# First 512 tokens as chunks of 128 and 384, in a fused polynomial-attention and rational-MLP kernel

## The chip, the cores and the metric

The kernel runs on one core of one Trainium2 chip. The metric is the device time of one execution in microseconds, taken as the median of several executions. The profile is of one further execution, recorded by the hardware profiler. The engines are PE (TensorE, matmuls into PSUM), ACT (ScalarE), DVE (VectorE), POOL (GpSimd) and SP (SyncE, which issues DMAs).

## The reference, cut to what matters

Four batches, four heads, 1088 positions and 32 features per head go through a linear attention with a product feature map, and the result (4352 tokens of 128 features) through a layer of 2048 hidden units with a rational activation.

```python
def phi(x):                                   # r = 8
    a = np.einsum('rd,bhsd->bhsr', S1, x)
    b = np.einsum('rd,bhsd->bhsr', S2, x)
    return np.einsum('bhsi,bhsj->bhsij', a, b).reshape(*x.shape[:-1], r * r)
q_p, k_p = phi(q), phi(k)
kv = np.einsum('bhsf,bhsd->bhfd', k_p, v);  z = np.sum(k_p, axis=2)
num = np.einsum('bhsf,bhfd->bhsd', q_p, kv)
den = np.einsum('bhsf,bhf->bhs', q_p, z)[..., None] + 1e-06
x = (num / den) transposed to (tokens, 128)
...
h = x @ w_in                                  # 128 -> 2048
P = a[0] + a[1]*h + a[2]*h**2 + a[3]*h**3
Q = 1.0 + abs(b[0])*abs(h) + abs(b[1])*h**2
out = (P / (Q + 1e-6)) @ w_out                # 2048 -> 128
```

## The kernel before, in words

**Order.** The kernel is a list of steps. `Plan.add` (line 67) notes for each step its engine, an estimated duration, what it comes after and which buffers it takes and gives back; `Plan.issue` (line 73) then issues the steps in the order of the hand-kept list `ORDER` (line 19). Every engine therefore works in the order in which its instructions come out of that list. An instruction that waits holds up all that stand behind it on its engine.

**Keys.** For each batch, `add_keys` (line 433) turns k into features: PE transposes (line 445), ACT copies the transposed keys from PSUM (449), PE projects them by S1 and S2 (454), ACT copies (461), DVE forms the products k_p (472). PE then sums k_p against v, with a column of ones for z (489). DVE spreads the sums into block matrices kv_bd and z_bd (544 to 552), PE projects z by S2 (557), and DVE writes the projected z into the third part of the query weights, W_abc for whole chunks (566) and W_rem for the remainder (563). W_abc has two places, used by batches of even and odd number.

**Queries.** `add_queries` (line 584) makes x for a chunk of tokens. Chunks have 512 tokens, two per batch, and one remainder chunk takes the last 64 positions of all four batches. The regular path: PE transposes q (595), ACT copies it (599), PE projects by W_abc to a, b and a third part c with which the denominator is a sum over eight products (605), ACT copies abc (615), DVE makes the denominator and scales a by its inverse (626, 630, 634, 638), then forms the products q_p (643), PE transposes them (651), ACT copies (657), PE multiplies by kv_bd straight into transposed x (663), ACT copies xT (712). Both chunks of a batch other than the first share one denominator pass.

The first 512 tokens go another way, as two chunks of 256 (labels 0 and 0b, the `early` branch). Their projection needs only S1 and S2, not z. After the product and its transposes, PE multiplies with the numerator and denominator columns of kv_bd side by side (676, with 1e-6 put in by 669), DVE inverts and divides (687, 693), PE transposes the result to x (701) and ACT copies xT (708). The loads of q for these two chunks come separately on SP (line 218).

**Hidden layer.** `add_group` (line 776) handles a group: one chunk and some of the 16 slices of 128 hidden units, up to 4096 columns in all (tokens times slices). PE makes h into PSUM tiles of 1024 columns (822; two such tiles exist), ACT, for some tiles DVE, casts it to bf16 into `hb` (828; `CASTS`, line 159, names groups whose seventh and eighth slices DVE casts). On `hb` DVE takes the absolute value u (837) and the square lin (845; on ACT, 843, for groups whose plan has an s), then y = lin*a3 + a1 (849), y *= hb (855). Q adds lin to u; ACT forms 1/Q as exp(-ln(...)) through the tile L (859, 862). P adds lin + a0 (852) to y, then y *= u (855), and PE multiplies by w_out (875). The two additions run on DVE (907), or, for groups whose entry in `PLANS` (line 158) has Q or P, as an accumulating DMA that POOL issues (911). A z in the plan lets PE add a0 through a second product with w_out instead of line 852. The groups of chunk 0 are of 2, 2, 4 and 8 slices of 256 tokens (`FIRST`, line 156) and lie packed in one set of buffers; chunk 0b is one group of 16 slices; all other chunks of 512 tokens have two groups of 8 slices; the remainder chunk has 8, 4, 3 and 1 slices of 256 tokens (`LAST`).

**Buffers.** Line 178 counts them: three each of hb, u, lin and y, one L, three w_ps tiles in PSUM for the attention part, one each of qT, abc, q_p and den. w_out is loaded as float32 into the buffer of L (196, 261). ACT scales it to w_out_b, POOL to w_out_0 (426, 427), and L is given back after that.

`HOT` (line 162) lists matmuls on zeros that fill PE's gaps (1036); they stand in `ORDER` too.

Of the kernel before, what the change touches and what calls it, by code (L numbers as in the profile page):

```python
# [12 lines left out]
FP = mybir.dt.float32  # L13
BF = mybir.dt.bfloat16
# [109 lines left out]
def kernel(  # L124
# [36 lines left out]
    XWARM = (0, 0)  # L161
# [34 lines left out]
    w_out_l = tile_of(moe, "L", [128, LW], FP)[:, :NF * d_model]  # L196
    w_out_f = w_out_l.rearrange("p (n d) -> p n d", d=d_model)
# [8 lines left out]
    def load_main(eng, name, src, b, part=None):  # L206
# [7 lines left out]
        if name == "q_sb" and part is not None:  # L214
            flat = T[name, b].rearrange("p h j d -> p (h j d)")
            if part < 1:
                for i in (int(2 * part),):
                    QUEUE[eng].dma_start(out=flat[:, i * 256:(i + 1) * 256].rearrange("p (h j d) -> p h j d", h=H, j=2),
                                         in_=src[:, :, 2 * i:2 * i + 2, :])
# [57 lines left out]
    ld["q", 0] = load("SP", lambda e: load_main(e, "q_sb", q, 0, 0), 128, rank=-97.5, take=["kq"])  # L277
# [3 lines left out]
    ld["q", 0, 0.5] = load("SP", lambda e: load_main(e, "q_sb", q, 0, 0.5), 128, rank=-96.7)  # L281
# [4 lines left out]
    ld["wo"] = load("SP", load_wo, 800, rank=-93, take=["L"])  # L286
# [15 lines left out]
    mask4 = consts.tile([128, H], FP, name="mask4")  # L302
    mask2 = consts.tile([128, 2], FP, name="mask2")
# [16 lines left out]
    den_e = consts.tile([128, 2, 4, 2], FP, name="den_e")  # L320
# [60 lines left out]
    c_s2 = plan.add("POOL", 250, s_expanded, after=[ld["s"], c_pool], rank=-3)  # L381
    c_sw = {}
# [48 lines left out]
    plan.add("DVE", 1, lambda: None, after=c_w + c_w0, rank=-0.1, give=["L"])  # L431

    def add_keys(b, rank):
# [141 lines left out]
        zs = plan.add("DVE", 200, lambda: z_spread(False), after=[zp, c_sw[b % 2]], rank=rank + 0.05, name=f"zspread {b}")  # L575
# [8 lines left out]
    def add_queries(n, nt, srcs, weights, kv_lhs, load_steps, kv_steps, w_steps, rank, give=(), early=False,  # L584
# [23 lines left out]
        def evac_abc():  # L608
# [5 lines left out]
            if nt == JC or early:  # L614
# [52 lines left out]
        def den_eps(t):  # L667
            T["nd", n, t] = tile_of(aps, "w_ps", [128, CW], FP)
            nc.tensor.matmul(nd_parts(t)[0][:, :, 2 * D:], lhsT=ident,
                             rhs=den_t[n % BUFS["den"]][:, 0:8, R].rearrange("p (g h) -> p g h", h=2), start=True, stop=False,  # L670
                             skip_group_check=True)

        def num_den(t, hp):
            for i in range(2):
                j = 2 * t + i
                nc.tensor.matmul(T["nd", n, t][:, (i * NP + hp) * 66:(i * NP + hp + 1) * 66],
                                 lhsT=T["q_pT", n][:, hp, j * 128:(j + 1) * 128],
                                 rhs=kv_lhs(hp)[0][2], start=False, stop=True, skip_group_check=True)

        def nd_parts(t):  # L680
            nd = T["nd", n, t][:, :4 * 66].rearrange("p (g c) -> p g c", g=4)
            den = den_e[:, n]
            return nd, den

        def div_inverse(t):
# [386 lines left out]
```

## Time and profile before

| | |
|---|---|
| median of 3 runs | 248.33 us (248.24 to 248.41) |
| the profiled execution | 248.28 us |
| its span, first to last instruction | 246.3 us |
| granted TensorE clock | 1.000 |
| busy: PE, DVE, ACT, POOL | 238.5, 222.9, 222.8, 55.0 us |
| POOL's DMA queue, share of 16 engines' span | 69.3% |

The span is from the first to the last instruction; the execution has some 2 us around it. A line of a timeline gives the start and the duration in microseconds, the engine, the line of the source, the operation, output and inputs with their shapes, how many instructions are merged (an f32 matmul that isn't a transpose appears as two passes), and in brackets the idle time of the engine before it with what ended it. A line of groups gives the busy time in us and the mean ns of one after the first bar, and after the second the idle time ahead of the group. Durations of instructions that follow each other on an engine overlap slightly, so start to start is the better measure for a row of them.

### The profile page before, as it was taken

To read this page: it belongs to the slowest core of one execution; us is meant where nothing else is said; L and a number is where in the kernel's file an instruction comes from. 1 tells how busy PE (TensorE), PEld (TensorE's weight loads), DVE (VectorE), ACT (ScalarE), POOL (GpSimd) and SP (SyncE) were. 2 spreads that over 40 slices of the span, in tenths; PEclk is the share of its full clock that TensorE was granted. 3 is DMA by queue.
4 is the path that set the end of the run, shared out by engine and by line. 5 is a ranking of instruction groups with operands and counts; after the bars stand their busy time and mean duration, and the time that the engine had idled before them with its cause. 6 is when DMAs were issued, how large, how long until landed. Compare 5 with 4: busy or idle time off the path is not lost. (4 is left out here: it accounts for less than half of the span.)

```text
span 246.3 us, 3019 instructions
## 1 busy us (share of the span) xinstructions
PE 238.5 (97%) x1119; PEld 140.3 (57%) x1129; DVE 222.9 (90%) x239; ACT 222.8 (90%) x201; POOL 55.0 (22%) x69
## 2 busy tenths in 40 slices
PE   7999999999999999999999999999999999999985
PEld 3889987566648556545654554444444446644442
DVE  0743898999999999999999999999999999999982
ACT  3236799989999999999999989999999999999993
POOL 7817000201130111151111112131132211111100
DMA  6897700497995498989999899999999999999742
GB/s 168 277 316 168 252 3 1 74 210 163 214 178 100 79 194 148 183 158 186 184 193 183 154 183 208 210 170 187 186 186 184 181 229 193 190 174 175 130 130 64
DMA packets 21662, 41.65 MB, mean 169 GB/s; under 512 B 5504, under 2 KB 12688, under 8 KB 21520
## 3 DMA queue, kind: packets, MB, share of 16 engines
q0 software_dynamic: 8000, 30.43, 69.3%
q1 hardware_dynamic: 13360, 10.95, 14.7%
q8 instruction: 9, 0.15, 0.3%
q10 hardware_dynamic: 288, 0.08, 0.2%
q14 instruction: 5, 0.04, 0.0%
HBM read 8.82 MB, written 2.23 MB: 45 GB/s over the span
## 5 line engine op out<-in xcount | busy, mean ns | idle before, releaser
L822 PE MATMUL h_ps<-xT,w_in_sb 128*128 128x512 f32 (+1 forms) x320 | 127.1, 534 | 0.7 <-ACT hb L828 0.7
L822 PEld LDWEIGHTS h_ps<-xT,w_in_sb 128*128 128x128 f32 x320 | 57.1, 190 | 42.3 <-issue 33.8
L828 ACT CAST hb<-h_ps 128x1024 bf16<-128x1024 f32 (+3 forms) x62 | 61.4, 1009 | 4.3 <-PE h_ps L822 4.0
L859 ACT ACTIVATE L<-u,kappa 128x4096 f32<-128x4096 bf16 (+5 forms) x23 | 65.0, 2830 | 0.3 <-DMA u<-lin 0.3
L862 ACT ACTIVATE u<-L 128x4096 bf16<-128x4096 f32 (+5 forms) x23 | 63.0, 2749 | 0.1
L911 POOL DMA_DIRECT2D u<-lin x16 | 22.3, 1395 | 99.8 <-DVE u L837 26.6
L855 DVE TENSOR_TENSOR y<-y,u 128x4096 bf16<-128x4096 bf16 (+5 forms) x23 | 39.6, 1729 | 0.9 <-ACT u L862 0.8
L855 DVE TENSOR_TENSOR y<-y,hb 128x4096 bf16<-128x4096 bf16 (+5 forms) x23 | 39.6, 1724 | 0.2
L845 DVE TENSOR_TENSOR lin<-hb 128x4096 bf16<-128x4096 bf16 (+5 forms) x22 | 37.3, 1702 | 2.2 <-ACT hb L828 2.1
L911 POOL DMA_DIRECT2D y<-lin x14 | 17.5, 1251 | 69.4 <-DVE lin L852 19.6
L875 PE MATMUL out_ps<-y,w_out_b 128*128 128x512 bf16 (+1 forms) x138 | 30.1, 354 | 1.4 <-DVE y L855 1.1
L849 DVE TENSOR_SCALAR y<-lin,a_t 128x4096 bf16<-128x4096 bf16 (+5 forms) x23 | 24.4, 1062 | 0.4 <-PE out_ps L875 0.3
L875 PEld LDWEIGHTS <-w_out_b 128*128 128x128 bf16 x144 | 14.0, 98 | 18.4 <-issue 7.0
L837 DVE TENSOR_SCALAR u<-hb 128x4096 int16<-128x4096 int16 (+5 forms) x23 | 21.6, 941 | 0.7 <-ACT hb L828 0.6
L489 PEld LDWEIGHTS w_ps<-v_aug,k_p 128*128 128x128 f32 x128 | 15.1, 192 | 2.5 <-issue 2.2
L489 PE MATMUL w_ps<-v_aug,k_p 128*128 128x96 f32 x128 | 15.6, 276 | 0.0
L852 DVE TENSOR_SCALAR lin<-lin,a_t 128x4096 bf16<-128x4096 bf16 (+5 forms) x17 | 15.3, 902 | 0.0
L657 ACT COPY q_pT<-w_ps 128x512 f32<-128x512 f32 (+1 forms) x20 | 10.5, 558 | 3.8 <-PE w_ps L651 3.8
L643 DVE TENSOR_TENSOR q_p<-abc 128x1024 f32<-128x1024 f32 (+1 forms) x10 | 10.6, 1062 | 1.1 <-ACT abc L615 1.0
L875 PE MATMUL out_ps<-u,w_out 128*128 128x512 bf16 x46 | 11.2, 379 | 0.3 <-ACT u L862 0.2
L472 DVE TENSOR_TENSOR k_p<-ab 128x1024 f32<-128x1024 f32 x8 | 9.8, 1234 | 1.7 <-ACT ab L461 1.7
L1036 PE MATMUL w_ps<-const-float32-0.0 128*128 128x512 bf16 x47 | 11.1, 381 | 0.1
(111 smaller groups left out, 221.1 us busy)
## 6 DMA issues: line engine op xcount, KB each, us to landing
u<-lin POOLq DMA_DIRECT2D x15, 1024.0 KB, 9.0
y<-lin POOLq DMA_DIRECT2D x13, 1024.0 KB, 8.9
v_aug<-in_v_dram SPq DMA_DIRECT2D x8, 256.0 KB, 4.2
out_dram<-oT SPq DMA_DIRECT2D x7, 256.0 KB, 5.2
kq<-in_k_dram SPq DMA_DIRECT2D x3, 512.0 KB, 4.3
kq<-in_q_dram SPq DMA_DIRECT2D x3, 512.0 KB, 7.1
w_in_sb<-in_moe_w_in_dram SPq DMA_DIRECT2D x1, 1024.0 KB, 6.0
kq<-in_k_dram SPq DMA_DIRECT2D x2, 256.0 KB, 3.3
```

The costliest lines, as they stand in the source:

```text
L489: nc.tensor.matmul(T["kv", b][:, hp * 96:(hp + 1) * 96], lhsT=lhs(hp), rhs=rhs(hp), start=(first and hp == 0), stop=final, skip_group_chec ...
L822: nc.tensor.matmul(T["h", g, s][:, i * W:(i + 1) * W], lhsT=w_in_sb[:, fi * 128:(fi + 1) * 128], rhs=T["xT", n][:, :W], start=True, stop=True)
L828: copy(out=T["t", g][:, s * W:(s + nsub) * W], in_=T["h", g, s][:, :nsub * W])
L837: nc.vector.tensor_scalar(out=u().bitcast(mybir.dt.int16), in0=ht().bitcast(mybir.dt.int16), scalar1=0x7FFF, scalar2=None, op0=AX.bitwise_and)
L845: nc.vector.tensor_mul(out=sq(), in0=ht(), in1=ht())
L849: nc.vector.tensor_scalar(out=y(), in0=sq(), scalar1=a_t[:, 3:4], scalar2=a_t[:, 1:2], op0=AX.mult, op1=AX.add)
L852: nc.vector.tensor_scalar(out=sq(), in0=sq(), scalar1=a_t[:, 0:1], scalar2=None, op0=AX.add)
L855: return lambda: nc.vector.tensor_mul(out=out(), in0=in0(), in1=in1())
L859: nc.scalar.activation(out=T["L", g][:, :gw], in_=u(), func=ACT.Ln, bias=1.0 + 1e-6, scale=kappa[:, 2:3])
L862: nc.scalar.activation(out=u(), in_=T["L", g][:, :gw], func=ACT.Exp, scale=-1.0)
L875: nc.tensor.matmul(T["o", n][:, :W], lhsT=w[:, fi, :], rhs=T[src, g][:, i * W:(i + 1) * W], start=(start and i == 0), stop=(stop and i == ...
L911: nc.gpsimd.dma_start(out=dst(), in_=src(), accum_op=AX.add, max_dma_last_dim=GW)
```

## The change

The first 512 tokens are split into 128 and 384. The 128 go the early way, now with one product, one division and one transpose. The 384 (label 0b) go the regular query path with their own denominator. Its weights need z of batch 0 for three 128-token columns only; they are put into batch 1's place of W_abc, with a mask built by POOL (`mask12`), and batch 1's own spread is ordered behind the projection of the 384 tokens. The q loads are 64 and 192 KB instead of twice 128 KB.

The groups change with the chunks: 4, 4 and 8 slices of 128 tokens, then two groups of 8 slices of 384 tokens (3072 columns), 512, 512, 1024, 3072 and 3072 columns where there were 512, 512, 1024, 2048 and 4096. A PSUM tile of h holds two slices of 384, each in a bank of its own, so a cast takes 768 columns. Group 3 adds Q and P by DMA, group 4 as before squares on ACT and adds both by DMA, group 8 adds only Q by DMA, and group 11 no longer casts on DVE. w_out is loaded into a buffer of y instead of L, and y is given back when both scalings are done. `ORDER` is a new list for all steps; `HOT` keeps its counts.

```diff
-    FIRST = [2, 2, 4, 8]
+    HEAD = 1
+    FIRST = [4, 4, 8]
     LAST = [8, 4, 3, 1]
-    PLANS = {**{g: "QP" for g in range(4, 20)}, 5:"Q",17:"Qz",**{g:"QPz" for g in (13,15,16,18)},4:"sQP",14:"QPz"}
-    CASTS = {18:(6,),16:(6,),14:(6,),12:(6,),17:(6,),13:(6,),15:(6,),11:(6,)}
+    PLANS = {**{g: "QP" for g in range(4, 20)}, **{g:"Q" for g in (5,8)},11:"QP",14:"QPz",17:"Qz",**{g:"QPz" for g in (13,15,16,18)},3:"QP",4:"sQP"}
+    CASTS = {18:(6,),16:(6,),14:(6,),12:(6,),17:(6,),13:(6,),15:(6,)}
...
-    w_out_l = tile_of(moe, "L", [128, LW], FP)[:, :NF * d_model]
-    w_out_f = w_out_l.rearrange("p (n d) -> p n d", d=d_model)
+    w_out_l = tile_of(moe, "y", [128, 2 * NF * d_model], BF)
+    w_out_f = w_out_l.bitcast(FP).rearrange("p (n d) -> p n d", d=d_model)
...
-    ld["q", 0] = load("SP", lambda e: load_main(e, "q_sb", q, 0, 0), 128, rank=-97.5, take=["kq"])
+    ld["q", 0] = load("SP", lambda e: load_main(e, "q_sb", q, 0, 0), 64, rank=-97.5, take=["kq"])
...
-    ld["q", 0, 0.5] = load("SP", lambda e: load_main(e, "q_sb", q, 0, 0.5), 128, rank=-96.7)
+    ld["q", 0, 0.5] = load("SP", lambda e: load_main(e, "q_sb", q, 0, 0.5), 192, rank=-96.7)
...
+    def pool_mask12():
+        nc.gpsimd.tensor_copy(out=mask12.rearrange("p h j -> p (h j)").rearrange("p (i m) -> p i m", m=H),
+                              in_=mask4[:, None, :].broadcast_to([128, JC - HEAD, H]))
...
-    plan.add("DVE", 1, lambda: None, after=c_w + c_w0, rank=-0.1, give=["L"])
+    plan.add("ST", 1, lambda: None, after=c_w + c_w0, rank=-0.1, give=["y"], name="used w_out")
...
+        def z_piece():
+            nc.vector.tensor_mul(
+                out=W_abc[:, 1, 0:JC - HEAD].rearrange("p i m r -> p (i m) r")[:, :, 2 * R:R3].rearrange("p (h j) r -> p h j r", h=H),
+                in0=T["zp", b][:, :H * R].rearrange("p (h i) -> p h i", h=H)[:, :, None, :].broadcast_to([128, H, JC - HEAD, R]),
+                in1=mask12[:, :, :, None].broadcast_to([128, H, JC - HEAD, R]))
+
+        if b == 0:
+            T["w_step", "piece"] = zp = plan.add("DVE", 170, z_piece, after=[zp, c_sw[1], c_m12], rank=rank + 0.05, name="zpiece")
+        zs = plan.add("DVE", 200, lambda: z_spread(False), after=[zp, c_sw[b % 2], T["q abc", 1] if b == 1 else None], rank=rank + 0.05, name=f"zspread {b}")
...
+        def both_transposes():
+            T["qpTp", n] = tile_of(aps, "w_ps", [128, CW], FP)
+            qp = T["q_p", n][:, :H, :].rearrange("p h f -> p (h f)")
+            for hp in range(NP):
+                nc.tensor.transpose(T["qpTp", n][:, hp * 128:(hp + 1) * 128], in_=qp[:, hp * 128:(hp + 1) * 128], identity=ident)
...
-                nc.tensor.matmul(T["h", g, s][:, i * W:(i + 1) * W], lhsT=w_in_sb[:, fi * 128:(fi + 1) * 128],
+                nc.tensor.matmul(T["h", g, s][:, i * step:i * step + W], lhsT=w_in_sb[:, fi * 128:(fi + 1) * 128],
                                  rhs=T["xT", n][:, :W], start=True, stop=True)
...
+            if step == W:
+                copy(out=T["t", g][:, s * W:(s + nsub) * W], in_=T["h", g, s][:, :nsub * W])
+            else:
+                copy(out=T["t", g][:, s * W:(s + nsub) * W].rearrange("p (i w) -> p i w", w=W),
+                     in_=T["h", g, s][:, :nsub * step].rearrange("p (i w) -> p i w", w=step)[:, :, :W])
...
-    chunks[0:1] = [(0, 0, j, 2) for j in range(0, JC, 2)]
+    chunks[0:1] = [(0, 0, 0, HEAD), (0, 0, HEAD, JC - HEAD)]
...
-        sizes = FIRST if n == 0 else (LAST if rem else [NF] if n == 1 else [GF] * (NF // GF))
+        sizes = FIRST if n == 0 else (LAST if rem else [GF] * (NF // GF))
...
-            early = nj < JC
+            early = n == 0
```

In the new order, PE's list after the early chunk's transpose to x is: q transposes of the next chunk, the 16 h matmuls of the 128 tokens, the q_p transposes of the 384 tokens, the next chunk's projection, four key transposes, the x product of the 384 tokens, four key projections, then the h matmuls of the 384 tokens with key and query work between them. ACT's list there is: xT, qT, abc of the 384 tokens, the first cast of h, half of w_out_b, q_pT, the second cast, q_pT, abc of the next chunk, kT, xT of the 384 tokens, the third cast, the other half of w_out_b, and casts of 768.

More of the change, by code (lines that the diff above doesn't have):

```diff
@@ L285 @@
     second = dict(mains(1))
-    ld["wo"] = load("SP", load_wo, 800, rank=-93, take=["L"])
+    ld["wo"] = load("SP", load_wo, 800, rank=-93, take=["y"])
     ld["k", 1] = load("SP", second["k"], 512, 1, rank=-91, take=["kq"])
@@ L381 @@
     c_s2 = plan.add("POOL", 250, s_expanded, after=[ld["s"], c_pool], rank=-3)
+    c_m12 = plan.add("POOL", 100, pool_mask12, after=[c_pool], rank=-98.9, name="mask12")
     c_sw = {}
@@ L664, in x_mm @@
                                      rhs=T["q_pT", n][:, hp, c0:c1], start=True, stop=True)
[L667 to L670, printed above, removed]
-                             skip_group_check=True)
[L673 to L678, printed above, removed]
@@ new lines, in both_evac, with nd_of, den_eps @@
+        def both_evac():
+            T["q_pT", n] = tile_of(att, "q_pT", [128, NP, CW], FP)
+            nc.scalar.copy(out=T["q_pT", n][:, :, :W], in_=T["qpTp", n][:, :NP * W].rearrange("p (n w) -> p n w", n=NP))
+        def nd_of():
+            return T["nd", n][:, :NP * 66].rearrange("p (g c) -> p g c", g=NP)
+        def den_eps():
+            T["nd", n] = tile_of(aps, "w_ps", [128, CW], FP)
+            nc.tensor.matmul(nd_of()[:, :, 2 * D:], lhsT=ident,
+                             rhs=den_t[0][:, 0:H, R].rearrange("p (g h) -> p g h", h=2), start=True, stop=False,
+                             skip_group_check=True)
@@ new lines, in num_den, with div_inverse, divide @@
+        def num_den(hp):
+            nc.tensor.matmul(T["nd", n][:, hp * 66:(hp + 1) * 66], lhsT=T["q_pT", n][:, hp, :W],
+                             rhs=kv_lhs(hp)[0][2], start=False, stop=True, skip_group_check=True)
+        def div_inverse():
+            nc.vector.reciprocal(out=den_e, in_=nd_of()[:, :, 2 * D:])
+        def divide():
+            T["x", n] = tile_of(moe, "o_sb", [128, CW], FP)[:, :128]
+            nc.vector.tensor_mul(
+                out=T["x", n].rearrange("p (g h d) -> p g h d", g=NP, h=2),
+                in0=nd_of()[:, :, 0:2 * D].rearrange("p g (h d) -> p g h d", h=2),
+                in1=den_e[:, :, :, None].broadcast_to([128, NP, 2, D]))
@@ L710, in x_evac, with x_transpose @@
+        def x_transpose():
+            T["xTp", n] = tile_of(aps, "w_ps", [128, CW], FP)
+            nc.tensor.transpose(T["xTp", n][:, :128], in_=T["x", n], identity=ident)
         def x_evac():
@@ L718, in rest @@
             T["prod", n] = s
+            if early:
+                s = plan.add("PE", 275, both_transposes, after=[s], rank=rank + 0.03, take=["w_ps"], give=["q_p"], name=f"qp tr {lab(n)},0")
+                s = plan.add("ACT", 270, both_evac, after=[s], rank=rank + 0.03, take=["q_pT"], give=["w_ps"], name=f"qp ev {lab(n)},0")
+                t = plan.add("PE", 120, den_eps, after=[c_pool], rank=rank + 0.04, take=["w_ps"], name=f"eps {lab(n)},0")
+                for hp in range(NP):
+                    t = plan.add("PE", 250, lambda hp=hp: num_den(hp), after=[t, s, kv_steps[0][hp]], rank=rank + 0.04,
+                                 give=["q_pT"] if hp == NP - 1 else [], name=f"nd {lab(n)},0,{hp}")
+                s = plan.add("DVE", 100, div_inverse, after=[t], rank=rank + 0.04, name=f"div inv {lab(n)},0")
+                s = plan.add("DVE", 210, divide, after=[s], rank=rank + 0.04, take=["o_sb"], give=["w_ps"], name=f"div {lab(n)},0")
+                s = plan.add("PE", 150, x_transpose, after=[s], rank=rank + 0.05, take=["w_ps"], give=["o_sb"], name=f"x tr {lab(n)},0")
+                return plan.add("ACT", ev, x_evac, after=[s], rank=rank + 0.05, take=["xT"], give=["w_ps"], name=f"x ev {lab(n)},0")
             pe = []
@@ L749, in rest @@
+            s = plan.add("PE", 700 if nt == BP else 278 * nt, x_mm, after=pe + kv_steps, rank=rank + 0.04,
+                         take=["w_ps"], give=["q_pT"], name=f"x mm {lab(n)}")
             return plan.add("ACT", ev, x_evac, after=[s], rank=rank + 0.05, take=["xT"], give=["w_ps"], name=f"x ev {lab(n)}")
         s = plan.add("PE", 110 * nt, transposes,
-                     after=load_steps + [c_id] + [T.get(("q tr", n - 1)) if give or early else None], rank=rank, take=["w_ps"],
+                     after=load_steps + [c_id] + [T.get(("q tr", n - 1)) if give else None], rank=rank, take=["w_ps"],
@@ L755, in add_queries @@
         s = plan.add("ACT", ev, evac, after=[s], rank=rank, take=["qT"], give=["w_ps"], name=f"q ev {lab(n)}")
-        s = plan.add("PE", 216 * (4 if nt == JC else 2 if early else B), project, after=[s] + w_steps, rank=rank + 0.01, take=["w_ps"],
+        s = plan.add("PE", 216 * (B if nt == BP else nt), project, after=[s] + w_steps, rank=rank + 0.01, take=["w_ps"],
                      give=["qT"], name=f"q abc {lab(n)}")
+        T["q abc", n] = s
         s = plan.add("ACT", 45 + G * RC * 109 // 128, evac_abc, after=[s, T.get(("eva", n - 1)) if pair == 1 else None], rank=rank + 0.01,
```

77 lines of the change are left out of this document (15 added, 62 removed), and 71 rows, old and new, of the table ORDER.

## The prediction

> **What bounds the kernel now.** I read the page's totals first, then the table by stages, cut where the roles of the engines change, then the timelines of the start.
>
> ```profile
> span 246.3 us, 3019 instructions
> PE 238.5 (97%) x1119; PEld 140.3 (57%) x1129; DVE 222.9 (90%) x239; ACT 222.8 (90%) x201; POOL 55.0 (22%) x69
> ```
>
> VectorE (DVE) and ScalarE (ACT) carry the same load, 222.9 and 222.8 us of 246.3; each is idle for some 23.4 us. PE's 97% is no limit in itself: pipelined matmuls count while they wait. The span is therefore the work of DVE or ACT plus its idle time, and the question is where those 23.4 us lie.
>
> ```profile
> core 0: us, PE busy (x) PEld busy (x) DVE busy (x) ACT busy (x) POOL busy (x), PEclk, DMA share, GB/s
> 0.00:21.10 21.10, 19.06 (x124) 15.16 (x125) 8.38 (x34) 7.64 (x17) 13.10 (x39) 1.00 0.90 261
> 21.10:40.85 19.75, 19.75 (x122) 17.04 (x121) 15.71 (x30) 17.01 (x25) 2.10 (x1) 1.00 0.34 91
> 40.85:60.00 19.15, 19.15 (x93) 12.03 (x91) 18.89 (x28) 18.08 (x20) 2.73 (x2) 1.00 0.59 129
> 60.00:225.00 165.00, 163.71 (x693) 87.94 (x699) 163.78 (x123) 162.69 (x129) 36.23 (x27) 1.00 0.97 178
> 225.00:246.30 21.30, 16.81 (x97) 8.10 (x97) 16.16 (x27) 17.38 (x15) 0.88 (x1) 1.00 0.54 118
> ...
> 0.00:24.02 24.02, 21.98 (x141) 17.78 (x142) 9.10 (x37) 9.98 (x21) 15.19 (x39) 1.00 0.86 237
> 24.02:50.00 25.98, 25.98 (x146) 20.22 (x145) 24.15 (x41) 23.82 (x30) 1.52 (x1) 1.00 0.32 85
> ```
>
> The first number after the stage is its length; length less busy time is idle time. ACT: 13.46 us idle up to 21.10, 2.74 up to 40.85, 1.07 up to 60, 2.31 in the 165 us up to 225, 3.92 in the tail. DVE: 14.92 us up to 24.02, 1.83 up to 50. From 60 to 225 both are 99% busy. So only three things can move the end: the idle time of the start (ACT 16.2 us by 40.85, DVE 16.75 by 50), the amount of work on the two engines, and the tail. The tail (LAST, the remainder chunk) keeps its groups and almost its order; I give it nothing. At 21.10 stands the first cast of h, at 24.02 DVE's first operation on it, at 40.85 ACT's square, which needs the last cast of the first 512 tokens:
>
> ```profile
> 17.12 0.37 ACT L708 COPY xT<-w_ps 128x256 f32<-128x256 f32 x1 [0.61 <-PE w_ps L701]
> 17.57 0.59 ACT L599 COPY qT<-w_ps 128x512 f32<-128x512 f32 x1
> 18.05 1.15 ACT L426 ACTIVATE w_out_b<-L,a_c 128x1024 bf16<-128x1024 f32 x1
> 21.10 1.02 ACT L828 CAST hb<-h_ps 128x1024 bf16<-128x1024 f32 x1
> 40.85 3.62 ACT L843 ACTIVATE lin<-hb 128x4096 bf16<-128x4096 bf16 x1
> ...
> 24.02 1.23 DVE L845 TENSOR_TENSOR lin<-hb 128x2048 bf16<-128x2048 bf16 x1 [2.06 <-ACT hb L828]
> ```
>
> **Part 1, the work.** The columns stay 8192 for these 512 tokens: 512, 512, 1024, 2048 and 4096 become 512, 512, 1024 and twice 3072. Where a 4096 and a 2048 form give way to two of 3072 on one line, the midpoint makes it nothing. What does not cancel:
>
> ```profile
> L828 ACT CAST hb<-h_ps 128x1024 bf16<-128x1024 f32 x58 | 59.1, 1036 | 2.7 <-PE h_ps L822 2.4
> L828 ACT CAST hb<-h_ps 128x768 bf16<-128x768 f32 x1 | 0.8, 798 | 0.0
> L843 ACT ACTIVATE lin<-hb 128x4096 bf16<-128x4096 bf16 x1 | 3.6, 3617 | 0.0
> L828 DVE CAST hb<-h_ps 128x1024 bf16<-128x1024 f32 x8 | 9.7, 1219 | 0.2 <-PE h_ps L822 0.2
> L845 DVE TENSOR_TENSOR lin<-hb 128x4096 bf16<-128x4096 bf16 x14 | 32.0, 2284 | 0.1
> L845 DVE TENSOR_TENSOR lin<-hb 128x2048 bf16<-128x2048 bf16 x2 | 2.4, 1222 | 2.1 <-ACT hb L828 2.1
> L907 DVE TENSOR_TENSOR y<-y,lin 128x4096 bf16<-128x4096 bf16 x2 | 4.6, 2288 | 0.0
> L907 DVE TENSOR_TENSOR y<-y,lin 128x2048 bf16<-128x2048 bf16 x1 | 1.2, 1219 | 0.0
> L907 DVE TENSOR_TENSOR u<-u,lin 128x2048 bf16<-128x2048 bf16 x1 | 1.2, 1217 | 0.0
> L626 DVE TENSOR_TENSOR den<-abc 128x64 f32<-128x64 f32 x1 | 0.2, 218 | 0.0
> ```
>
> ACT: five casts of 1024 fewer (5 x 1.04 = 5.2 us), eight of 768 more (8 x 0.80 = 6.4), so +1.2: one cast comes over from DVE (CASTS loses 11), and the padded PSUM tiles hold 768 columns where they held 1024. The square shrinks from 4096 to 3072 columns, 3.62 x 1/4 = -0.9. Sum **ACT +0.3**. DVE: the cast -1.2; the square of one 3072 group instead of one 2048 group, 1.75 (midpoint of 2.28 and 1.22) - 1.22 = +0.5; the two adds of the old 2048 group go (-1.22 - 1.22), their heirs go by DMA, and group 8's P comes back to DVE (+2.29), together -0.1; the four small denominator operations for the 384 tokens +1.0 (12 groups each, estimate from 0.22 for 8) and the weight piece +0.3, against a second division with its reciprocal, some 0.7 (estimates, all operations of this small class): +0.6. Sum **DVE -0.2**. The accumulating DMAs move the same number of columns (before 28 x 4096, after 25 x 4096 and 4 x 3072, and 2 x 2048 in both). PE loses some 1 us of small matmuls.
>
> **Part 2, the start.** PE's rows give the price of a pass (an f32 matmul counts as two):
>
> ```profile
> 19.66 1.03 PE L605 MATMUL w_ps<-W_abc,qT 128*128 128x96 f32 x8
> 20.53 1.92 PE L822 MATMUL h_ps<-xT,w_in_sb 128*128 128x256 f32 x8
> ...
> 30.17 5.45 PE L822 MATMUL h_ps<-xT,w_in_sb 128*128 128x256 f32 x24
> 35.46 1.04 PE L651 MATMUL w_ps<-ident,q_p 128*128 128x128 f32 x8
> ...
> 47.79 3.60 PE L822 MATMUL h_ps<-xT,w_in_sb 128*128 128x512 f32 x8
> 51.22 0.60 PE L595 MATMUL w_ps<-ident,kq 128*128 128x128 f32 x4
> ```
>
> From start to start: 96 columns 0.87/8 = 0.11 us, 256 columns 5.29/24 = 0.22, 512 columns 3.43/8 = 0.43. The trace has no f32 pass of 128 columns: it lies between 0.11 and 0.22, nearest to 96; I take 0.12. 384 columns: 0.325, the midpoint.
>
> The Trainium skill ("TensorE: Matmul & The Clock Gate", section "LDWEIGHTS (loading the stationary operand)") times a weight load by its columns, 128 / 1.2 = 107 ns, however few columns stream past. The 0.11 us of the 96-column pass agrees. By the page a 128-column pass is bound by its load at 0.107, an estimate, the 32 of them take 3.4 us, and the sum below would be 246.8.
>
> Now follow the new order. The one 128-token chunk reaches xT at about the same time as now (17.1): fewer transposes and divisions ahead of it save a few tenths, the zpiece on DVE and the three transposes and projections of the 384 tokens, put ahead on PE, take them back. Then PE runs h for 16 x 128 columns: 32 x 0.12 = 3.8 us, 17.25 to 21.1. ACT copies qT of the next chunk and the 384 tokens' abc (to 18.2), casts the first 512 columns at 18.2 (**2.9 us sooner than now**), scales half of w_out until 19.85, and then waits about 1.65 us, because the transposes of q_p stand behind all 16 h matmuls on PE. From 21.5 it copies q_pT, h, q_pT, abc and kT almost without a gap; PE passes q abc, four key transposes and the x product, so xT of the 384 tokens comes at 24.0. Behind it PE has 8 key passes and 32 h passes of 0.325 = 10.4 us with 1.7 us of transposes between: 24.8 to 36.8. ACT follows at PE's pace with gaps of 0.35, 0.45 and 0.5 us up to 29.2, then is full: L, exp, casts, copies. The last cast ends at 38.1 and the square begins at **38.3** instead of 40.85. Adding the busy pieces I find ACT busy for 23.5 of 38.3 us, idle for 14.8 against 16.2: **-1.4 us**. DVE starts on h at 20.3, waits at 20.7 to 22.5 for the second cast and at 36.6 to 38.4 for the second key half of batch 1; idle by 50 about 14.2 against 16.75: **-2.5 us**.
>
> What else moves: the loads of q are 64 and 192 KB instead of twice 128 in the same places on SP, so v lands earlier by the time of 64 KB, and nobody waits for q. w_out in a buffer of y: ACT and POOL must have scaled it before the fourth tile of y is taken, group 4's, at about 46. ACT's half is done at 26.3 by the reckoning above, and of POOL the trace says:
>
> ```profile
> 7.44 3.48 POOL L376 COPY W_abc<-S 128x64 f32<-128x64 f32 x4
> 17.53 5.67 POOL L427 TENSOR_SCALAR w_out<-L,a_sb 128x1024 bf16<-128x1024 f32 x2 [6.25 <-DMA L<-in_moe_w_out_dram]
> ```
>
> It is through at 23.2, so nothing waits, and L, which is set free, was not waited for either: no gain, no loss. Batch 1's weights (the place that the 384 tokens borrow) are overwritten only after batch 1's keys, long after the projection at 16. The new mask copy stands on POOL ahead of the weight copies that end at 10.9; the piece is needed at 15.4.
>
> **The sum.** ACT: -1.4 idle, +0.3 work, later gaps as now: -1.1. DVE: -2.5 and -0.2, -2.7, so it gets slack and ACT sets the end. The profiled execution took 248.28 us (1.98 around its span of 246.3); 248.28 - 1.1 = **247.2**, and the median of the runs (248.33) lies so near that I leave it.
>
> **The rivals.**
>
> *DVE's slack helps ACT too.* If part of ACT's 2.31 us between 60 and 225 is DVE being late and the rest of the order closes the start's gaps better than my reading, the gain nears DVE's 2.7: 245.6. For: both engines feed each other in every group. Against: ACT's waits in that stage are for PE's h_ps.
>
> *The first DMA add becomes the wait.* Group 3 adds Q by DMA, issued at about 35.4, when DMA is free; ACT's L of group 3 could start at about 44.6.
>
> ```profile
> u<-lin POOLq DMA_DIRECT2D x15, 1024.0 KB, 9.0
> u<-lin POOLq DMA_DIRECT2D x1, 512.0 KB, 5.0
> ```
>
> 3072 columns lie between 5.0 and 9.0 us: landing at 40.4 to 44.4, just in time. From 9.2 us on every us is lost, and at 10.3 the gain is gone: 248.2, no change. The share of 0.34 up to 40.85 speaks against it; the same sort of loss in other gaps that I read as closed counts here too.
>
> *Slower: the 128-column passes hold up the 384 tokens.* Sixteen h matmuls stand ahead of the q_p transposes, on which xT, all 3072-column groups and ACT's casts hang. If a pass of 128 costs what one of 256 does, 0.22, the 16 take 7.0 instead of 3.8 us and everything behind comes 3.2 us later: 247.2 + 3.2 = 250.4. It decides from 0.155 a pass (32 x 0.035 = 1.1). For: h is written to fresh PSUM and each pass brings a new weight. Against: the 96-column row.
>
> **How the numbers follow.** Forecast 42% (its own range 246.5 to 247.8), DVE's slack 16%, DMA or other gaps 17%, slower 25%. A measurement of this kernel tells 0.2%, 0.5 us, from no change: faster 0.42 + 0.16 = 0.58, same 0.17, slower 0.25. The range goes from 245.2, just below the best rival, to 249.4, which takes in the lesser half of the slower one.
>
> **What would show it.** First cast at about 18.2 us and DVE's first operation on h at about 20.3; ACT's square at 38.3; two gaps on ACT before 24; 32 passes of 128 columns in 3.8 us; ACT busy 223.1, DVE 222.7; ACT more than 98% busy from 40 to 225. I am wrong if the square of group 4 begins after 39.7, or if both engines show new gaps between 40 and 100, where the order is new and I only carried over the old gaps.

## The result, and the profile after

The changed kernel takes 249.42 us (median of 7 runs, 248.84 to 250.12), the kernel before 248.41 beside it (7 runs): ratio 1.0035, 95% interval 1.0018 to 1.0052. It is **0.35% slower**, 0.9 to 1.0 us. 247.2 was forecast. The profiled execution took 250.12 us, the longest of its seven, 1.84 us more than the profiled execution of before; a part of what its rows show is therefore not in the medians, which differ by 1.0. Its k landed late (first copy of kT at 5.29 us, 4.73 in before), but that was made up for by 13 us: ACT copies q_pT at 12.94 and xT at 17.12, in before at 12.92 and 17.12. That copy of xT moves from profile to profile, 16.66 to 17.48 us over the ten profiles here that have the new start, so half a microsecond between two profiles is no effect of a change.

The page's totals after, then the table by stages of after and, for the stages that the prediction did not show, of before (columns as in the prediction's table):

```profile
span 248.3 us, 3003 instructions
PE 238.2 (96%) x1116; PEld 136.8 (55%) x1116; DVE 223.6 (90%) x240; ACT 222.8 (90%) x203; POOL 54.6 (22%) x71
```

```profile
0.00:40.00 40.00, 38.24 (x229) 28.97 (x230) 25.07 (x69) 24.43 (x44) 16.68 (x41) 1.00 0.68 191
40.00:60.00 20.00, 20.00 (x111) 13.01 (x111) 17.57 (x25) 18.07 (x18) 3.57 (x3) 1.00 0.99 211
60.00:100.00 40.00, 38.77 (x174) 21.73 (x173) 39.65 (x31) 36.95 (x36) 6.01 (x5) 1.00 0.71 126
100.00:225.00 125.00, 125.00 (x510) 64.99 (x509) 123.88 (x90) 123.98 (x94) 27.28 (x21) 1.00 0.96 177
225.00:248.30 23.30, 16.18 (x97) 8.07 (x95) 17.44 (x29) 19.37 (x16) 1.04 (x2) 0.93 0.56 115
```

```profile
0.00:40.00 40.00, 37.96 (x236) 31.35 (x237) 23.86 (x63) 23.83 (x40) 15.19 (x39) 1.00 0.64 182
40.00:60.00 20.00, 20.00 (x100) 12.88 (x99) 19.12 (x29) 18.90 (x21) 2.73 (x2) 1.00 0.57 123
60.00:100.00 40.00, 39.95 (x197) 24.22 (x197) 39.51 (x30) 39.49 (x36) 6.83 (x5) 1.00 0.83 155
100.00:225.00 125.00, 123.76 (x497) 63.72 (x502) 124.26 (x94) 123.20 (x94) 29.41 (x22) 1.00 1.01 185
```

Work did not change (ACT 222.8 both times), so the span is idle time again. Stage length less busy time, for ACT, with two experiments beside it (e2 holds batch 3's loads back, e7 also swaps two ACT operations; both below):

| ACT idle, us | before | after | e2 | e7 |
|---|---|---|---|---|
| 0 to 40 | 16.17 | 15.57 | 15.54 | 15.05 |
| 40 to 60 | 1.10 | 1.93 | 1.92 | 1.92 |
| 60 to 100 | 0.51 | 3.05 | 1.70 | 1.55 |
| 100 to 225 | 1.80 | 1.02 | 1.00 | 0.45 |
| 225 to the end | 3.92 | 3.93 | 3.94 | 3.93 |

The start gained 0.6 us, 40 to 100 lost 3.4, and 100 to 225 gained 0.8: together the 2.0 us between the spans. The granted clock of 0.93 in the last stage of after costs nothing that these rows show, since ACT is idle there for 3.93 us against 3.92. DVE shows where it began: 40 to 60 has 2.43 us idle after, 0.88 before. The start came out much as forecast. The timeline of after (start, duration, operation; in brackets the idle time before it):

```profile
17.44 3.84 PE L827 MATMUL h_ps<-xT,w_in_sb 128*128 128x128 f32 x32
...
18.64 0.58 ACT L834 CAST hb<-h_ps 128x512 bf16<-128x512 f32 x1
...
22.02 0.48 ACT L675 COPY q_pT<-w_ps 128x384 f32<-128x384 f32 x1 [1.75 <-PE w_ps L669]
...
38.94 2.85 ACT L852 ACTIVATE lin<-hb 128x3072 bf16<-128x3072 bf16 x1
...
21.30 0.42 DVE L854 TENSOR_TENSOR lin<-hb 128x512 bf16<-128x512 bf16 x1
```

The 32 passes of 128 columns take 3.84 us, the cast comes 2.5 us sooner than before and the square 1.9 sooner. Two places behind it are new:

```profile
51.43 2.81 ACT L871 ACTIVATE u<-L 128x3072 bf16<-128x3072 f32 x1
...
56.13 1.76 DVE L864 TENSOR_TENSOR y<-y,u 128x3072 bf16<-128x3072 bf16 x1 [1.49 <-ACT hb L834]
...
87.26 0.18 DVE L561 TENSOR_TENSOR z_bd<-w_ps,mask 128x32 f32<-128x32 f32 x1
...
87.50 0.41 PE L566 MATMUL w_ps<-z_bd,S2x 128*128 128x32 f32 x2 [1.23 <-DVE z_bd L561]
...
90.13 1.01 ACT L834 CAST hb<-h_ps 128x1024 bf16<-128x1024 f32 x1 [1.13 <-PE h_ps L827]
...
97.30 0.48 ACT L633 COPY abc<-w_ps 128x384 f32<-128x384 f32 x1 [1.19 <-PE w_ps L623]
```

**Place 1**, DVE at 54.64 to 56.13. The bracket names ACT, but group 3's exp (the row at 51.43) was done at 54.24. What ends the wait is the other input: group 3's P, added to y by an accumulating DMA that POOL issued at 45.35. The DMA view of after, for what was issued from 45 to 50 and, behind the dots, from 50.5 to 56, with the issue on POOL, the load issues on SP, and, behind the dots, those of before:

```profile
y<-lin POOLq DMA_DIRECT2D x1, 768.0 KB, 10.7
kq<-in_k_dram SPq DMA_DIRECT2D x1, 512.0 KB, 6.5
...
y<-lin POOLq DMA_DIRECT2D x1, 768.0 KB, 11.3
```

```profile
45.35 1.18 POOL L920 DMA_DIRECT2D y<-lin  x1 [2.05 <-DVE lin L861]
45.14 0.37 SPq L226 DMA_DIRECT2D kq<-in_k_dram  x1
45.56 2.27 SPq L212 DMA_DIRECT2D v_aug<-in_v_dram  x2
51.44 0.37 SPq L226 DMA_DIRECT2D kq<-in_q_dram  x1
...
51.85 0.37 SPq L224 DMA_DIRECT2D kq<-in_k_dram  x1
52.27 1.20 SPq L210 DMA_DIRECT2D v_aug<-in_v_dram  x2
60.74 0.37 SPq L224 DMA_DIRECT2D kq<-in_q_dram  x1
```

The last number of a row of the DMA view is the time in us from issue to landing. 45.35 and 10.7 is 56.05. Batch 3's k, v and q go out as soon as their buffers are free. Before, that was at 51.85, 52.27 and 60.74; with the faster start and the new order it is 6.7 to 9.3 us sooner, beside the adds of P of groups 3 and 4.

**Place 2**, PE at 86.3 to 87.5: z_bd of chunk 2 stands on DVE behind two operations of 4096 columns, and PE, in order, holds h back from ACT.

### The profile page after: what moved, and what is told of

The parts are those of the page before. It is cut to its first block, busy times and chain, and to the rows that moved or that the text cites. A ratio compares the mean times of both kernels' runs of the same rounds, so it can differ in the third digit from the quotient of the medians.

```text
span 248.3 us, 3003 instructions
## 1 busy us (share of the span) xinstructions
PE 238.2 (96%) x1116; PEld 136.8 (55%) x1116; DVE 223.6 (90%) x240; ACT 222.8 (90%) x203; POOL 54.6 (22%) x71
## 5 line engine op out<-in xcount | busy, mean ns | idle before, releaser
L827 PE MATMUL h_ps<-xT,w_in_sb 128*128 128x512 f32 (+3 forms) x320 | 125.6, 534 | 0.0
L868 ACT ACTIVATE L<-u,kappa 128x4096 f32<-128x4096 bf16 (+6 forms) x23 | 65.5, 2852 | 0.9 <-DMA u<-lin 0.9
L871 ACT ACTIVATE u<-L 128x4096 bf16<-128x4096 f32 (+6 forms) x23 | 63.7, 2774 | 0.1
L864 DVE TENSOR_TENSOR y<-y,u 128x4096 bf16<-128x4096 bf16 (+6 forms) x23 | 39.7, 1731 | 3.4 <-ACT u L871 1.8
L864 DVE TENSOR_TENSOR y<-y,hb 128x4096 bf16<-128x4096 bf16 (+6 forms) x23 | 39.7, 1728 | 0.1
L854 DVE TENSOR_TENSOR lin<-hb 128x4096 bf16<-128x4096 bf16 (+6 forms) x22 | 37.8, 1726 | 1.3 <-ACT hb L834 1.3
L884 PE MATMUL out_ps<-y,w_out_b 128*128 128x512 bf16 (+2 forms) x144 | 30.6, 355 | 0.0
L858 DVE TENSOR_SCALAR y<-lin,a_t 128x4096 bf16<-128x4096 bf16 (+6 forms) x23 | 24.4, 1063 | 0.3
L846 DVE TENSOR_SCALAR u<-hb 128x4096 int16<-128x4096 int16 (+6 forms) x23 | 21.9, 954 | 0.2
L861 DVE TENSOR_SCALAR lin<-lin,a_t 128x4096 bf16<-128x4096 bf16 (+6 forms) x17 | 15.1, 894 | 0.1
L884 PE MATMUL out_ps<-u,w_out 128*128 128x512 bf16 x48 | 11.3, 379 | 1.4 <-ACT u L871 1.4
L661 DVE TENSOR_TENSOR q_p<-abc 128x1024 f32<-128x1024 f32 (+3 forms) x10 | 10.6, 1064 | 0.2
```

The costliest lines, as they stand in the source:

```text
L827: nc.tensor.matmul(T["h", g, s][:, i * step:i * step + W], lhsT=w_in_sb[:, fi * 128:(fi + 1) * 128], rhs=T["xT", n][:, :W], start=True, st ...
L846: nc.vector.tensor_scalar(out=u().bitcast(mybir.dt.int16), in0=ht().bitcast(mybir.dt.int16), scalar1=0x7FFF, scalar2=None, op0=AX.bitwise_and)
L854: nc.vector.tensor_mul(out=sq(), in0=ht(), in1=ht())
L858: nc.vector.tensor_scalar(out=y(), in0=sq(), scalar1=a_t[:, 3:4], scalar2=a_t[:, 1:2], op0=AX.mult, op1=AX.add)
L861: nc.vector.tensor_scalar(out=sq(), in0=sq(), scalar1=a_t[:, 0:1], scalar2=None, op0=AX.add)
L864: return lambda: nc.vector.tensor_mul(out=out(), in0=in0(), in1=in1())
```

## Experiments

Theory A at first: the start gained, places 1 and 2 each lost some of it, independently. Rivals: B, the small chunk itself costs; C, one engine's slack covers the other's gap; D, the add is slow by itself. All ratios below are to the kernel before on the same chip; times of runs on different chips are compared through it.

**e1: z_bd forward** (place 2 undone).

```diff
-    ... 414, 468, 204, 451, 470, 46, 450, 205, 433, ...
+    ... 414, 468, 204, 205, 451, 470, 46, 450, 433, ...
```

> The changed kernel with one step moved in the order: the fill of z_bd of chunk 2 stands directly behind that of kv_bd of the same chunk, as in the kernel before, and no longer behind the lin and u operations of 4096 columns. Theory A (the start gained what was forecast, and the new order of the middle lost it in two new waits, of which this is one): the z projection of chunk 2 on PE no longer waits 1.23 us at 86.3 to 87.5, ScalarE's gaps at 90 and 97 (1.13 and 1.19 us) shrink to under 0.3 each, and the time comes out 1.2 to 2.3 us under the changed kernel's 249.42, at 247.1 to 248.2. Rival B (the small chunk itself costs: more instructions, slower passes, a crowded start; the waits in the middle are only where that debt shows): the gaps close here and open again later, time 249.0 to 249.6. Rival C (VectorE, not ScalarE, sets the end by now): ScalarE's gaps close, VectorE's busy time stays, time 248.9 to 249.5 with new ScalarE waits for y or for casts behind VectorE before 225.

Measured 249.65 us, ratio 1.0049 (1.0033 to 1.0065). No gain: theory A fails for place 2. ACT's wait of 1.13 at 90 is gone, but the one of 1.19 stays (now at 95.8), and 0.51 and 0.70 open 45 us later, as rival B had it (that the debt is not the chunk's own, e2 shows). The timeline of e1 (its line numbers are two lower):

```profile
135.77 1.01 ACT L832 CAST hb<-h_ps 128x1024 bf16<-128x1024 f32 x1 [0.51 <-PE h_ps L825]
137.49 1.01 ACT L832 CAST hb<-h_ps 128x1024 bf16<-128x1024 f32 x1 [0.70 <-PE h_ps L825]
...
55.85 1.76 DVE L862 TENSOR_TENSOR y<-y,u 128x3072 bf16<-128x3072 bf16 x1 [1.24 <-DMA y<-lin]
```

This execution also names the releaser of place 1: the DMA into y.

**e2: batch 3's loads held back** (place 1 without the neighbours of the add).

```diff
+        if name == "k_sb" and b == B - 1:
+            nc.vector.memset(T[name, b][:, 0, 0, 0:1], 0.0)
         js = slice(0, J) if part is None else slice(part * JC, part * JC + JC)
...
-    ... 423, 420, 406, 45, 177, ... 346, 389, 197, ...
+    ... 423, 420, 406, 177, ... 346, 389, 45, 197, ...
```

> The changed kernel with batch 3's loads of k, v and q held back: a one-element VectorE write into the k tile, put in the order behind group 4's last product, stands ahead of them, so that they go out at about 73 us and no longer at 45 to 51. Nothing else moves; the k loaded is first needed at about 94. Theory A: the DMA add of group 3's P, issued at 45.35, lands in 7.5 to 9 us and not in 11.0, the y product at 56.13 begins by 54.9, VectorE's idle time of 50 to 60 goes from 2.31 to under 1.2, and the time comes out 0.5 to 1.5 us under 249.42, at 247.9 to 248.9. Rival D (the add is slow by itself on its queue, whatever else the engines of the DMA carry): its landing stays at 10 to 11 us, the gap stays, time 249.1 to 249.7. Rival B or C: the gap closes and the time is still 249.0 to 249.6.

Measured 247.98 us, ratio 0.9978 (0.9968 to 0.9989): 1.4 us under the changed kernel, and under the kernel before. The same two windows of the DMA view in e2, the load issues, and the rows of both places:

```profile
q0 software_dynamic: 323, 0.94, 106.2%
...
y<-lin POOLq DMA_DIRECT2D x1, 768.0 KB, 7.7
...
y<-lin POOLq DMA_DIRECT2D x1, 768.0 KB, 6.4
```

```profile
71.89 0.37 SPq L226 DMA_DIRECT2D kq<-in_k_dram  x1
...
54.53 1.75 DVE L864 TENSOR_TENSOR y<-y,u 128x3072 bf16<-128x3072 bf16 x1
...
85.65 0.18 DVE L561 TENSOR_TENSOR z_bd<-w_ps,mask 128x32 f32<-128x32 f32 x1
...
86.07 0.30 PE L566 MATMUL w_ps<-z_bd,S2x 128*128 128x32 f32 x2
```

P of group 3 lands after 7.7 us instead of 10.7, P of group 4 after 6.4 instead of 11.3, and DVE does not wait. Place 2 closes too, with z_bd where the change put it: DVE reaches it 1.6 us sooner. (ACT's wait of 1.19 for abc stays, as in e1.) The two places had one cause. The first line (packets, MB, share of the 16 DMA engines' time) says why there is no room: in 45 to 50 the adds alone, two in flight, fill the 16 engines. The Trainium skill ("DMA: Bandwidth & Descriptors", section "Issuing engines are not separate DMA queues") says that DMAs issued by SP, ACT and POOL run on the same 16 DMA engines and interleave; these landings agree. Rival D falls, and B with it as far as these 1.4 us go.

**e3: both edits.**

```diff
-    ... 414, 468, 204, 451, 470, 46, 450, 205, 433, ...
+    ... 414, 468, 204, 205, 451, 470, 46, 450, 433, ...
...
+            nc.vector.memset(T[name, b][:, 0, 0, 0:1], 0.0)
```

> Both edits at once: z_bd of chunk 2 behind kv_bd, and batch 3's loads held back to about 73 us. Theory A: the two waits are of two engines and at two places, so the gains add: 1.7 to 3.0 us under 249.42, at 246.4 to 247.7, under the kernel before. Rival C (one engine's slack covers the other's gap): no better than the better of the two edits alone. Rival B: 249.0 to 249.6.

Measured 247.94 us, ratio 0.9974 (0.9963 to 0.9985), the same as e2, which rival C's time allows as well. Theory A's sum of two gains is refuted once more: there was one.

**e4: the changed kernel up to 57 us, from there the order of before.** ORDER is after's up to step 368 (group 3's last product), then before's sequence of the remaining steps, and its plans:

```diff
-    PLANS = {..., **{g:"Q" for g in (5,8)},11:"QP",14:"QPz",17:"Qz",...}
-    CASTS = {18:(6,),16:(6,),14:(6,),12:(6,),17:(6,),13:(6,),15:(6,)}
+    PLANS = {..., 5:"Q",17:"Qz",...,14:"QPz"}
+    CASTS = {18:(6,),16:(6,),14:(6,),12:(6,),17:(6,),13:(6,),15:(6,),11:(6,)}
```

> A hybrid: the changed kernel's chunks of 128 and 384, its place for the weights and w_out, and its order up to 57 us; from there the order of the kernel before, with that kernel's plans of what goes to GpSimd's DMA adds (group 8 again Q and P) and of the casts (group 11's again on VectorE). The loads of batch 3 stay early, so the wait at 54.6 to 56.1 should stay. Theory A (chunking good, new middle order bad): the waits of 87 to 97 are gone, 246.9 to 248.2, under the kernel before. Rival B (the chunking itself costs): 249.0 to 250. Rival E (the new balance of later groups was a gain that the old plans lose): 248.4 to 249.4, with more VectorE time and new waits behind 100.

Measured 248.48 us, ratio 1.0007 (0.9994 to 1.0019), in E's range alone, between A's and B's; of E's signs, ACT's idle time from 100 to 225 is there (2.18 us against 1.02 in after), more DVE time is not (222.4 against 223.6). Place 1 is there (1.22 us idle), and the time is that of before.

**e5 and e6: the same hold in e4, and as a control in the kernel before.** The hold stands again behind group 4's last product (step 389 in e5, 384 in e6).

> The hybrid (the changed kernel up to 57 us, from there the order and plans of the kernel before) with batch 3's loads held back as in the second run. Theory A, as it stands after four runs (the chunking and the start gain 0.9 to 1.4 us, and the early loads beside the DMA add of group 3 cost it 1.2 to 1.5 us again): the wait of 1.2 us at 54.6 goes here too, 247.0 to 247.4. Theory F (the new order of the middle is itself worth something, the old order of the middle loses it again): 247.7 to 248.5, with new VectorE gaps behind 60. Theory G (the held loads help only the new order, because there z_bd waits behind VectorE): 248.2 to 248.6.

> Control: the kernel before, with batch 3's loads held back in the same way, to behind group 4's last product (they went out at 51.85, 52.27 and 60.74 there). Theory A (the collision came with the change: before, the adds that those loads run beside have slack): 248.2 to 248.7, no gain. Rival (late loads are a gain for either kernel, so that the second run's 1.4 us tell nothing of this change): 247.0 to 247.9.

Measured: e5 249.85 us, ratio 1.0047 (1.0029 to 1.0066); e6 250.58 us, 1.0078 (1.0048 to 1.0108). Both **slower**, which no expectation had; the runs of e6 spread from 249.66 to 252.26. In the old order that product ends 8 us later, so the loads go out at 80 to 82, beside other adds. ACT in e6, and in before at the same place; then, in the DMA view, the u add that it waits for (issued at 87.76 in e6, 87.81 in before), first e6, then before:

```profile
98.84 3.72 ACT L860 ACTIVATE L<-u,kappa 128x4096 f32<-128x4096 bf16 x1 [1.73 <-DMA u<-lin]
```

```profile
97.04 3.76 ACT L859 ACTIVATE L<-u,kappa 128x4096 f32<-128x4096 bf16 x1
```

```profile
u<-lin POOLq DMA_DIRECT2D x1, 1024.0 KB, 11.0
```

```profile
u<-lin POOLq DMA_DIRECT2D x1, 1024.0 KB, 8.3
```

It is place 1 made afresh in another kernel: 2.7 us more for the add, 1.73 us of ACT, and 2.0 us of time. As controls these two failed; e6 is a second case of the mechanism.

**e7: e2 with one swap on ACT**, the cast of group 9's first pair of h ahead of the second half of chunk 4's numerators.

```diff
-    ... 212, 488, 215, 216, 489, 236, ...
+    ... 212, 488, 215, 489, 216, 236, ...
```

> The second run's kernel (loads held back) with one swap on ScalarE: at 94.6 the cast of group 9's first pair of h stands ahead of the second half of chunk 4's numerators, which waits there for PE 1.19 us. The cast's h is ready at about 94.8, so ScalarE's wait shrinks to 0.2 to 0.4. If ScalarE sets the end, 0.6 to 0.9 us under 247.98, at 247.1 to 247.4. If VectorE sets it (it has 1.4 us of idle time between 60 and 225, ScalarE 2.7), 247.8 to 248.1, with ScalarE's idle time coming back later as waits for VectorE.

Measured 247.73 us, ratio 0.9966 (0.9952 to 0.9980). The wait of 1.19 us shrinks to 0.32, but a wait of 0.73 for h opens at 96.3 behind it. The time lies between the two expectations; its interval and e2's overlap, so a gain over e2 is not shown.

**e8: only v and q held** (512 KB instead of 1.5 MB in the way).

```diff
+            if b == B - 1:
+                nc.vector.memset(v_aug[b % 2][:, 1, 0, 0:1], 0.0)
             for hp in range(NP) if part is None else (part,):
```

> A smaller dose: the changed kernel with only v and q of batch 3 held back (the one-element write goes to the v tile); k, 512 KB, still goes out at 45.1 beside group 3's DMA add of P. Theory A with rival b's threshold of the prediction (a landing up to 9.2 us costs nothing, each us behind it is lost): 512 KB less per 1 MB in the way, so the add lands in 8.5 to 9.3 us between the 7.0 of the second run and the 11.0 of the changed kernel, VectorE's wait at 54.6 is under 0.3, time 247.9 to 248.3. If the k load alone makes the collision (it is issued 0.2 us ahead of the add and shares its whole flight): landing 10 to 11, wait 1.0 to 1.5, time 249.0 to 249.6.

Measured 248.68 us, ratio 1.0001 (0.9990 to 1.0013), between the two. The two P adds in e8 and DVE's wait:

```profile
y<-lin POOLq DMA_DIRECT2D x1, 768.0 KB, 9.9
...
y<-lin POOLq DMA_DIRECT2D x1, 768.0 KB, 8.0
...
55.53 1.76 DVE L864 TENSOR_TENSOR y<-y,u 128x3072 bf16<-128x3072 bf16 x1 [0.50 <-ACT hb L834]
```

The dose answers: P of group 3 lands after 7.7, 9.9 and 10.7 us with none, k, and all beside it; DVE waits 0, 0.5 and 1.5 us; the time is 247.98, 248.68 and 249.42. The expectation had 8.5 to 9.3 for the landing and missed that k alone, which flies beside this add all the way, does most of the harm to it.

**e9 and e10: e5 and e6 put right**, with the hold behind the product q_p of chunk 3 (step 179 in e9, 180 in e10), so that the loads go out at 63.

> The fifth run put right: there the held loads went out at 79.9 (the old order has group 4's last product 8 us later), beside DMA adds that ScalarE then waited for at 97. Here the hybrid's one-element write stands behind the product q_p of chunk 3, so that batch 3's loads go out at about 63. If only that collision made the fifth run slow: VectorE's wait at 54.6 is gone, the wait for DMA at 97 is gone, 247.0 to 247.7. If the old order of the middle has a wait of its own behind it (the fifth run's trace shows VectorE 1.62 us idle at 60.4 for PE's transposes, where the fourth has 0.31): that wait stays at 1.4 to 1.7, it takes the place of the DMA wait, and the time is that of the fourth run, 248.2 to 248.8.

> Control, put right in the same way: the kernel before with batch 3's loads held to about 63 us (k and v went out at 52, q at 60.7). If late loads are no gain of their own and the sixth run was slow by its collision at 80 to 97 alone: 248.3 to 248.8, no change. If holding loads back helps any order: 247.2 to 247.9. If it harms any order but the new one: over 249.2.

Measured: e9 248.43 us, ratio 1.0001 (0.9991 to 1.0011); e10 249.28 us, 1.0034 (1.0021 to 1.0048). e9 lies in the second of its ranges. e10 lies in "harms any order but the new one", but the harm has a place: e10 meets yet another add: u, issued at 69.51, takes 12.3 us where it takes 8.8 in before, and DVE stands:

```profile
81.82 1.29 DVE L853 TENSOR_SCALAR lin<-lin,a_t 128x4096 bf16<-128x4096 bf16 x1 [1.12 <-DMA u<-lin]
```

So for the kernel before, batch 3's loads had the best of the three places tried. In e9 neither ACT nor DVE waits for a DMA up to 100, and yet there is no gain over before. DVE does not wait for P either (its product starts at 53.73 without a gap). From DVE's timeline of e9:

```profile
61.69 1.23 DVE L661 TENSOR_TENSOR q_p<-abc 128x1024 f32<-128x1024 f32 x1 [1.62 <-PE w_ps L669]
```

DVE waits 1.62 us for PE's transposes instead, where e4 had 0.31; the product begins at 61.69, in before at 61.75. The old order of the middle leaves PE where it was, so as far as these rows show the start's lead ends there. The new middle (e2 against e9, intervals apart) lets some of the lead through; order and plans were not separated, and e9's loads go out 9 us before those of e2.

**e11: e7 with PE's numerators of chunk 1 drawn forward**, to take ACT's 0.87 us at 43.2. (Only the moved steps and their neighbours are shown.)

```diff
-    153 (PE kv 1,1), 186 (PE k tr), 154 (PE kv rem 1), 140 (PE x mm 1)
+    153, 140, 186, 154
-    187 (ACT k ev), 141 (ACT x ev 1)
+    141, 187
-    155, 156 (DVE kv_bd, z_bd), 365, 335 (DVE lin)
+    365, 335, 155, 156
```

> The seventh run's kernel with one more wait of ScalarE taken away: chunk 1's numerator matmuls on PE stand ahead of a transpose of k and of the remainder of kv, their eviction to xT on ScalarE ahead of that of kT, and kv_bd and z_bd on VectorE behind two lin operations. ScalarE's wait of 0.87 us at 43.2 goes to 0.2 or less. If ScalarE still sets the pace there: 0.3 to 0.7 us under 247.73, at 247.0 to 247.4. If both engines are full behind it and VectorE's 1.9 us of early waits decide: 247.6 to 247.9.

Measured 248.52 us, ratio 0.9995 (0.9984 to 1.0005): 0.7 to 0.8 us worse than e7 and outside both expectations. The waits of 0.87 and 0.16 on ACT became three in e11:

```profile
43.53 0.59 ACT L725 COPY xT<-w_ps 128x512 f32<-128x512 f32 x1 [0.32 <-PE w_ps L681]
...
45.45 0.21 ACT L473 COPY ab<-w_ps 128x64 f32<-128x64 f32 x1 [0.78 <-PE w_ps L463]
...
48.82 0.59 ACT L617 COPY qT<-w_ps 128x512 f32<-128x512 f32 x1 [0.41 <-PE w_ps L623]
```

and DVE's wait for abc at 51 grew from 0.90 to 1.07. That explains some 0.5 us by the rows. Near 217 ACT's wait for a DMA add into u is 0.94 in e11's profile and 0.37 in e7's, but the first is the longest of its runs and the second the shortest. Why the median lost 0.7 to 0.8 stays open.

## Why the prediction was wrong

**The start: right in its course, smaller in size.** First cast forecast at 18.2, measured 18.64 (18.2 to 19.0 over the ten profiles with this start); square 38.3 against 38.94 (38.1 to 39.3); DVE's first operation on h 20.3 against 21.30, of which 0.74 is the stretched operation told at the end; ACT's long wait for the transposes 1.65 against 1.75; 32 passes 3.8 against 3.84. ACT's idle time up to 40 fell by 0.6 in this execution; 1.4 was forecast. Over the ten profiles it is 14.7 to 16.0, with a mean of 15.4, and over the three with the old start (before, e6, e10) 16.1 to 16.5, with a mean of 16.3: a gain of 0.9. DVE's idle time up to 50 fell by 1.0 to 1.7; 2.5 was forecast. The slower rival (a 128-column pass at 0.22) is dead: 0.12 was measured.

**The work: right for ACT** (222.8 against 223.1). DVE's 223.6 against 222.7 is not the change: runs with the same DVE work show 222.5 to 223.7.

**"Later gaps as now": the step that failed.** The sum carried the old gaps over from 40 us on. ACT's idle time from 40 to 100 grew by 3.4 us, from 100 to 225 it fell by 0.8. The prediction's own last sentence named this as what would make it wrong; its chances and its range, which ended at 249.4, did not make room for a loss that outweighs the start. 1.4 us of the loss is the wait for group 3's P (e2). "So it gets slack", said of DVE, failed with it: DVE's wait of 1.5 us was not taken up by any slack, it went through to the end.

**The rival "the first DMA add becomes the wait": right mechanism, wrong add, wrong price.** It looked at group 3's Q, which lands in time in every run. The wait was for P, the second add of the same group. Its bound for a landing, 5.0 to 9.0 us, came from medians: single adds of 1024 KB in before landed after 7.9 to 13.0 us. One of them, the y add issued at 62.13 beside batch 3's q, took 10.6 (8.7 in e6, where that load is gone), and nothing waited for it. And its evidence against, a DMA share of 0.34 up to 40.85, was of the old timeline: an earlier start frees the load buffers earlier too, and 40 to 60 went from 0.57 to 0.99. Its form of a threshold held for P, which must land 9.3 to 9.5 us after its issue (45.35 and 54.64, when DVE is free, in after; 45.56 and 55.02 in e8): 7.7 cost nothing, 9.9 cost 0.5, 10.7 cost 1.5 us of DVE. The price was then about one to one, 1.4 us of time in e2, and nothing behind the wait took it up: DVE's idle time from 60 to 225 is 1.47 us in after and 1.37 in e2.

**What is left.** Without the collision the change gains 0.2% (e2, 0.45 to 0.55 us), not the 1.1 us of the forecast. A part of what is missing is the start's gain, 0.9 for 1.4. Against it stand ACT's new waits behind 40 us, in e2 these (for a DMA, as in the third row, ACT waits at most 0.27 in before):

```profile
44.54 0.59 ACT L725 COPY xT<-w_ps 128x512 f32<-128x512 f32 x1 [0.87 <-PE w_ps L681]
...
95.76 0.48 ACT L633 COPY abc<-w_ps 128x384 f32<-128x384 f32 x1 [1.19 <-PE w_ps L623]
...
217.72 3.71 ACT L868 ACTIVATE L<-u,kappa 128x4096 f32<-128x4096 bf16 x1 [0.90 <-DMA u<-lin]
```

Removing the wait at 94.6 (e7) gave at most 0.25, and removing that at 43.7 (e11) lost. Which of them sets the end was not settled.

## What to carry to other kernels

When a change makes a stage faster, list what its buffers release: loads that are issued on release move with it, and may land beside a transfer that something waits for. Judge a DMA's landing by what flies beside it in the new timeline, not by its median in the old one. Here 1.5 MB of loads beside accumulating DMAs cost 0.9 to 2.0 us at three places (45, 63 and 80 us) where an engine waited for the add, and nothing at others where none did. Of two new waits downstream, remove the earlier one first: the later one may be the same microsecond.

## What the runs showed of the hardware

An f32 DVE operation with two inputs that began soon after the start of a GpSimd scaling was stretched, as if it had begun only 0.95 to 1.0 us after GpSimd's start, in each of five profiles. In after:

```profile
18.31 6.04 POOL L436 TENSOR_SCALAR w_out<-y,a_sb 128x1024 bf16<-128x1024 f32 x2 [7.25 <-DMA y<-in_moe_w_out_dram]
...
18.53 1.00 DVE L644 TENSOR_TENSOR den<-abc 128x96 f32<-128x96 f32 x1 [1.93 <-ACT abc L633]
```

The same operation takes 0.97 us in e11 (GpSimd starts at 18.28, the operation at 18.54), 0.53 in e7 (17.70 and 18.39) and 0.43 in e4 (18.10 and 18.88). In the six other profiles with this start it begins 0.98 us or more behind GpSimd, which starts at 16.9 to 17.5, and takes 0.26. In one of the six, e8, it is the product q_p that is stretched, 1.67 us for 0.96, when it begins at 20.09, 0.3 us after GpSimd's second scaling. A bf16 operation was not: in after, lin at 21.30 begins some 0.15 us after the second scaling and takes its usual 0.42. The stretch did not move the end of the start: DVE's second operation on h begins at 23.02 in after and at 22.99 in e2.

The Trainium skill ("SBUF — State Buffer", section "Who interferes with whom") says that a DVE instruction with two inputs in SBUF contends with a GpSimd instruction that reads it, and calls the shared port pair an exclusive lock; that the other engine blocks for the whole instruction it says of DVE's 2-port modes. The contention agrees with the f32 rows and not with the bf16 one. A block for the whole instruction would not agree: GpSimd's two instructions last 2.85 and 3.20 us in after, and DVE was let go after about 1.0. Spans on GpSimd are rough, and no run was made for this.
